# Layer-norm means, variances, reciprocal roots and shifts moved to GpSimd

## The chip, the cores and the metric

The kernel runs on one core of a Trainium2 chip. The metric is the device time of one launch in microseconds; the runs of the kernel before have a median of 207.16 us (206.71 to 207.61, two runs). The core has five engines that follow their own instruction queues in order and wait for each other by semaphores: TensorE (PE, matrix products), VectorE (DVE), ScalarE (ACT), GpSimd (POOL), and SyncE (SP), which issues the DMAs here.

## The reference

A block with a conditioned layer norm, a local dilated attention and a token-mixing MLP, on x of 2048 tokens by 512 channels in bf16. Shortened:

```python
def _layernorm(x, axis=-1, eps=1e-05):
    m = jnp.mean(x, axis=axis, keepdims=True)
    v = jnp.var(x, axis=axis, keepdims=True)
    return (x - m) / jnp.sqrt(v + eps)

mod = (silu(c) @ w_mod)            # six rows of 512: sa, ca, ga, sb, cb, gb
h = _layernorm(x) * (1 + ca) + sa                       # layer norm 1 (LN1)
x = x + ga * A(h, wqkv, wo)        # 32 heads of 16, 8 keys each, two tokens apart
h = _layernorm(x) * (1 + cb) + sb                       # layer norm 2 (LN2)
x = x + gb * B(h, w1, b1, w2, b2)

def B(x, ...):
    h = _layernorm(x)                                   # layer norm 3 (LN3)
    u = gelu(einsum('bsd,sf->bdf', h, w1) + b1)         # mixes the 2048 tokens, f = 1792
    return transpose(einsum('bdf,fs->bds', u, w2) + b2)
```

## The kernel before

The 2048 tokens are 16 tiles of 128 (token in the partition, 512 channels in the row), in five chunks of 2, 4, 4, 4 and 2 tiles (`SIZES`, so chunks begin at tiles 0, 2, 6, 10 and 14). For each chunk there is LN1, a transpose of the normalised tiles (by PE for the first two chunks, by DMA for the others: `xt`), the three projections (`qkv`, with evictions `ev`), the products of queries and keys on DVE (`qk`, four multiplies of 4096 columns for a chunk of four tiles), their sums by PE (`red`), a softmax (`max`, `sub`, `exp`, `esum`, `rcp`, `smB`), the products with the values on DVE (`pv`, four multiplies of the same size, summed by PE in `pvacc`), and the output projection with the residual (`wo`, `x1`). Then come LN2 (`n2_<tile>`), its affine part on DVE (`aff`, two multiplies or adds over the whole group) and LN3 (`h3_<tile>`). The products of `qk` and `pv` lie in four buffers named big, which `red` and `pvacc` release.

The MLP's first product (`mlp1_<sweep>_<feature tile>_<first token tile>`) sums over token tiles. It runs in sweeps over tiles 0 to 5, 6 to 10 and 11 to 15 for the feature tiles 0 to 6, and over tiles 0 to 9 and 10 to 15 for the feature tiles 7 to 13. A sweep's sums wait in `gT` (`park`, `inj`, `padd`) until the next. After GELU the second product (`mlp2`) and the output (`fin`, `st_out`) follow.

Each piece of work is added to a graph (`G.add`), with an engine, what it reads and what it writes. A list written out by hand, `ORDER`, gives the order in which all pieces are issued; so each engine's queue is the list's pieces of that engine, in the list's order. Nearly every instruction is issued through one helper, which is why the profile gives line 133 for all.

A layer norm's small work goes as follows. `ln_stats` (line 370) takes a tile's statistics: `bn_stats` and an aggregate on DVE (`ln1s`, `ln2s`, `ln3s`), or, for LN1 of tiles 10 to 13, two ACT sums and one DVE instruction (`ln1v`). LN2 of tiles 0 to 13 has its sums from ACT's `x1` and `ln2q`, and DVE makes the variance with two instructions (`ln2m`, line 869). `ln_rstd` (line 387) works on a group of tiles at a time: ACT takes Ln and Exp of the variance (`rstd`), DVE the shift (`nb`). A group is a whole chunk for LN1; for LN2 and LN3 it is 2, 2, 4, 1 and 1 tiles in the five chunks (`GRP`), and its name is that of its first tile (`rstd2_4`, `rstd3_4`). `ln_norm` (line 404) applies the scale and the shift on the engine that `NE` names for each tile, A for ACT, D for DVE, P for POOL:

```python
NE=('PAPAAPAADAAPAAPD', 'PAPAAPAAAADAAADP', 'APPAAADDDDADAADA'),
```

POOL has little else to do: constants and halos, two scalings of weights (`wsc2_2`, `wsc2_3`) and these normalisations. The parts of `ORDER` that matter most for the layer norms of the first tiles, of the first LN2 groups, and of the last tiles (lines 184, 208 to 209 and 222 to 224):

```
ln1s2 warm2 ld_wqkv0 silu_exp ld_wmod0 ln1s0 ln1s4 ln1s1 ln1s5 rstd1_0 ld_x_4_14 nb1_0 ln1s9 rstd1_1 n1_0 n1_1
...
warm3 n2_2 ev4_10:a ln3s0 wo6 a2_3_0 n2_3 ln3s1 a2_3_1 rstd2_4 wo7 x1_6 vd3_1 aff2 rstd3_0 a2_3_2 biascols wo9:q
ev4_20:a a2_3_3 nb2_4 nb3_0 ln3s3 n2_5 n2_4 vd3_2 warm1 ln3s2 h3_1 h3_0 qkv4_12 aff4 rstd3_2 wo8 x1_7 ld_w2_0
...
mlp1_0_13_0 aff10 oev4_0:a oev4_2:a aff13 mlp1_0_13_4 ln3s10 wo15 ld_w2_5 ln3s13 rstd3_10 mlp1_0_13_8 wo14 x1_15
rstd3_13 park0_12:a inj1_0 nb3_13 ln2s15 mlp1_1_0_6 nb3_10 x1_14 rstd2_15 mlp1_1_4_6 park0_13:a nb2_15 ln2s14
n2_15 inj1_3 inj1_6 ld_w1_1_896 inj1_5 mlp1_1_6_6 rstd2_14 aff15 h3_10 mlp1_1_3_6 ln3s15 mlp1_1_6_10 ln3s11
```

Of the kernel before, what the change touches and what calls it, by code (L numbers as in the profile page):

```python
# [8 lines left out]
ALU = mybir.AluOpType  # L9
BF = mybir.dt.bfloat16  # L10
F32 = mybir.dt.float32
PSUM = bass.MemoryType.PSUM
# [7 lines left out]
EPS = 1e-5  # L20
MASKVAL = -1.0e9
# [161 lines left out]
consts ld_x_1_2 act_table ld_x0 ld_x_1_4 ld_c ld_x_2_8 ld_x1 ident ld_x_2_6 ld_wmod1 ln1s3 halo0 ld_wqkv1 cps  # L183
ln1s2 warm2 ld_wqkv0 silu_exp ld_wmod0 ln1s0 ln1s4 ln1s1 ln1s5 rstd1_0 ld_x_4_14 nb1_0 ln1s9 rstd1_1 n1_0 n1_1
silu_dve nb1_1 ld_wqkv2 ln1s8 fill:2:70 tr0_0 n1_2 n1_4 modcols1 ln1s7 hT0_3:a n1_5 n1_3 ld_x_3_10 hT0_2:d a1col
hT0_0:a fill:4:16 tr1_2 wsc1_2:d ld_b1 hT0_1:a wsc1_3:d wsc1_0:a tr1_0 wsc1_1:d ln1s6 hT1_2:a ld_wmod2 qkv0_10
ld_x_3_12 wsc0_0:d rstd1_2 wsc0_1:d qkv0_12 wsc0_2:d hT1_1:a nb1_2 n1_8 n1_9 wsc0_3:d modcols0 hT1_0:d ld_wmod3
hT1_3:a qkv0_00 sab ev0_12:d n1_6 ld_wmod4 qvb0 ln1s14 ld_wo1 qkv0_02 qvb_cp0 ln1s15 ev0_00:a wsc2_2 qvb1
wsc2_0:d qkv1_00 wsc2_3 ev0_10:a ev0_02:d ln1s10 wsc2_1:d qkv1_10 qvb_cp1 qk0_0 ev1_10:a qkv0_22 qk0_1 n1_7
qkv0_20 ln1s13 qk0_2 qkv1_02 xt6 red0_0 ev1_00:a qk0_3 red0_1 red0_2 ev0_22:a ld_wmod5 qkv1_22 qk1_0 ev0_20:a  # L190
qkv1_12 ev1_02:a vd0_1 red0_3 ev1_12:a mask qkv1_11 vd0_0 ln1s11 max0 xt8 qk1_2 qkv1_01 ev1_11:a sub0 qkv1_03
ev1_01:a xt9 exp0 qkv1_13 qk1_1 ev1_03:a xt7 esum0 ev1_13:a qkv1_20 rcp0 vd0_2 ln1s12 qkv1_21 smB0 qk1_3 a2_0_3
modcol2 rstd1_4 qkv1_23 a2_0_0 ev1_22:a a2_0_2 halo_v1:a red1_0 ev1_20:a a2_0_1 red1_1 ln1v10 ln1v12 ln1v11
ln1v13 nb1_4 red1_2 rstd1_3 n1_15 ld_wo3 red1_3 nb1_3 ld_wo2 mcols0 n1_11 n1_10 qkv2_00 max1 ev1_21:a n1_14 xt10
qkv2_02 ev2_00:a pv0_0 qkv2_10 n1_12 ld_wo0 pv0_1 qkv2_11 vd0_3 ev2_10:a ev2_02:a qkv2_12 qk2_0 n1_13 qkv2_01
xt12 ev2_12:a pvacc0_0 ev2_01:a sub1 qk2_2 xt13 qkv2_03 exp1 qkv2_13 xt11 ev2_11:a ev2_03:a qkv2_22 qk2_1
ev2_13:a esum1 ev1_23:a qkv2_21 rcp1 vd1_2 red2_0 smB1 ev2_21:a ld_b2 red2_1 qk2_3 halo_v2:a a2_1_1 red2_2
pvacc0_1 a2_1_3 qkv3_00 a2_1_2 qkv3_10 a2_1_0 pv0_2 mrowt0 vd1_1 qkv2_20 ev3_10:a pv0_3 ev3_00:a red2_3 mrows0:a
qkv2_23 ev2_20:a st_row0 max2 halo_k3:p ev2_22:a vd1_3 qkv3_11 qk3_0 xt14 qkv3_22 ev3_11:a pvacc0_2 ld_row0
pvacc0_3 sub2:q oev0_2:a vd1_0 pv1_2 qkv3_02:q exp2 qkv3_12 ev3_02:a ev2_23:a qkv3_01 pv1_3 oev0_0:a vd2_2 esum2  # L200
modcol3 xt15 rcp2 ev3_12:a woq_s qkv3_20 ev3_01:a pvacc1_3 smB2 ev3_20:a red3_0 qk3_1 ev3_22:a a2_2_0 pvacc1_2
wo1 a2_2_1 vd2_3 qkv3_13:q x1_1 a2_2_2 pv1_1 vd2_1 wo0 ev3_13:a a2_2_3 qkv4_02 ld_w1_0_512 oev1_2:a mcols1 pv1_0
ld_w1_0_0 oev1_3:a mrowt1 qkv3_03 mrows1:a x1_0 st_row1 qkv4_00 ev3_03:a vd2_0 ln2q1 qk3_2 pvacc1_0 ev4_02:a
red3_1 pvacc1_1 oev1_0:a qkv3_23:q oev1_1:a qk3_3 ev4_00:a wo3:q ln2q0 wo5:q pv2_2 qkv4_22:q x1_5 ev3_23:a wo2:q
ld_row1 ln2q5 ld_w1_0_896 ln2m0 halo_v3:a wo4:q x1_3 pv2_1 x1_2 red3_2 x1_4 red3_3 ln2q3 qkv3_21:q pv2_3 rstd2_0
qkv4_20 ln2q2 ev3_21:a ev4_22:a vd3_3 pvacc2_1 nb2_0 max3 pvacc2_2 n2_0 warm0 ln2q4 vd3_0 n2_1 ln2m2 sub3 pv2_0
pvacc2_3 oev2_2:a exp3 rstd2_2 esum3 oev2_1:a aff0 pvacc2_0 rcp3 oev2_0:a qkv4_10 oev2_3:a ln2m4 nb2_2 smB3
warm3 n2_2 ev4_10:a ln3s0 wo6 a2_3_0 n2_3 ln3s1 a2_3_1 rstd2_4 wo7 x1_6 vd3_1 aff2 rstd3_0 a2_3_2 biascols wo9:q
ev4_20:a a2_3_3 nb2_4 nb3_0 ln3s3 n2_5 n2_4 vd3_2 warm1 ln3s2 h3_1 h3_0 qkv4_12 aff4 rstd3_2 wo8 x1_7 ld_w2_0
nb3_2 ln3s5 h3_3 h3_2 ln2q6 ln3s4 mlp1_0_6_0 ev4_12:a pv3_0 mlp1_0_3_0 x1_9 rstd3_4 mlp1_0_5_0 x1_8 mlp1_0_0_0  # L210
biascols_cp:a ln2q8 nb3_4 pv3_1 halo_v4:a mlp1_0_2_0 h3_4 vd4_1 h3_5 mlp1_0_1_0 ln2q9 pv3_2 ld_w2_1 mlp1_0_2_4
vd4_2 ln2q7 mlp1_0_0_4 vd4_0 mlp1_0_3_4 park0_0:a mlp1_0_1_4 mlp1_0_5_4:q park0_1:a ln2m6 vd4_3 pv3_3 park0_2:a
pvacc3_0 pvacc3_1 oev3_0:a ld_w1_0_1152 pvacc3_2 oev3_1:a mlp1_0_4_0:q rstd2_6 oev3_2:a qk4_2 pvacc3_3 park0_3:a
mlp1_0_7_0 oev3_3:a nb2_6 qk4_1 n2_6 mlp1_0_6_4 mlp1_0_4_4 n2_8 qk4_0 wo12:q ld_w1_0_1408 n2_7 n2_9 qk4_3 wo10:q
park0_4:a aff6 x1_12 red4_0 wo13:q ld_w2_3 park0_5:a ln2q12 red4_1 red4_2 x1_10 red4_3 wo11:q max4 ln2q10 ln3s9
x1_13 sub4:q mlp1_0_8_0:q exp4 ln3s8 ln2q13 mlp1_0_11_0 esum4 ln3s7 rcp4 mlp1_0_12_0 park0_6:a ln3s6 x1_11
mlp1_0_10_0 smB4 rstd3_6 ln2m12 a2_4_2 mlp1_0_9_0 h3_7 rstd2_12 h3_6 a2_4_3 ln2q11 h3_9 mlp1_0_8_4 ln2m13 a2_4_0
nb2_12 ln2m11 n2_12 mlp1_0_7_4 a2_4_1 ln2m10 h3_8 rstd2_10 ld_w2_4 aff12 mlp1_0_9_4 rstd2_13 rstd2_11 nb2_10
ln3s12 mlp1_0_9_8 mlp1_0_7_8 n2_10 mlp1_0_8_8 nb2_13 pv4_0 park0_7:a mlp1_0_12_4 ld_w1_0_1664 park0_8:a
mlp1_0_11_4 nb2_11 pv4_2 n2_13 mlp1_0_10_4 rstd3_12 pv4_1 park0_9:a mlp1_0_12_8 n2_11 mlp1_0_10_8 pv4_3 inj1_4  # L220
mlp1_0_11_8 ld_w1_1_0 park0_10:a pvacc4_2 ld_w1_1_640 park0_11:a pvacc4_0 nb3_12 aff11 pvacc4_1 h3_12 pvacc4_3
mlp1_0_13_0 aff10 oev4_0:a oev4_2:a aff13 mlp1_0_13_4 ln3s10 wo15 ld_w2_5 ln3s13 rstd3_10 mlp1_0_13_8 wo14 x1_15
rstd3_13 park0_12:a inj1_0 nb3_13 ln2s15 mlp1_1_0_6 nb3_10 x1_14 rstd2_15 mlp1_1_4_6 park0_13:a nb2_15 ln2s14
n2_15 inj1_3 inj1_6 ld_w1_1_896 inj1_5 mlp1_1_6_6 rstd2_14 aff15 h3_10 mlp1_1_3_6 ln3s15 mlp1_1_6_10 ln3s11
mlp1_1_0_10 rstd3_15 inj1_1 mlp1_1_1_6 park1_0:a nb3_15 h3_15 n2_14 rstd3_11 aff14 mlp1_1_5_6 h3_13 ln3s14
mlp1_1_5_10 mlp1_1_1_10 inj1_2 ld_w1_2_0 mlp1_1_2_6 h3_11 rstd3_14 park1_1:a h3_14 mlp1_1_4_10 mlp1_1_3_10
mlp1_1_2_10 mlp1_1_9_10 park1_2:a ld_w1_1_1408 park1_3:d mlp1_1_7_10 padd1_9 park1_4:a park1_5:d mlp1_1_8_10
padd1_7 gelu7 mlp1_1_10_10 park1_6:a mlp1_2_2_11 ld_w1_2_640 padd1_10 mlp1_2_2_14 mlp1_2_0_11 padd2_2
mlp1_2_0_14 ld_w2_7 gelu2 mlp1_2_1_11 padd2_0 mlp1_2_1_14 gelu0 mlp1_1_12_10 padd2_1 gelu10 padd1_8 gelu1
# [4 lines left out]
st_out5_0 fin8_0 mlp2_2_0 fin9_0 mlp2_13_0 fin2_0 st_out9_0 st_out8_0 st_out2_0 fin7_0 mlp2_10_0 fin13_0  # L234
st_out7_0 fin6_0 mlp2_12_0 st_out6_0 st_out13_0 mlp2_11_0 fin12_0 fin10_0 st_out12_0 mlp2_14_0 st_out10_0
fin11_0 st_out11_0 mlp2_15_0 fin14_0 mlp2_15_1 st_out14_0 fin15_0 mlp2_15_2 fin15_1 st_out15_0 st_out15_1
fin15_2 st_out15_2
# [4 lines left out]
def kernel(  # L242
# [92 lines left out]
    epscol = T([P, 1], F32, "epscol")  # L335
# [17 lines left out]
    for l in range(3):  # L353
        for nm, n in (("st6", 6), ("mv", 2), ("lv", 1), ("rs", 1), ("nb", 1)):
            ln_t[nm, l] = T([P, NST, n], F32, f"{nm}_{l}")
# [14 lines left out]
    def ln_stats(l, st, src, reads, name):  # L370
        st6, mv = ln_t["st6", l], ln_t["mv", l]
        if l == 0 and st in LN1A:
            def fa():
                nc.scalar.activation(junk[:], src, ACT.Identity, scale=1.0 / D, accum_out=mv[:, st, 0:1])
                nc.scalar.activation(junk[:], src, ACT.Square, scale=D ** -0.5, accum_out=st6[:, st, 0:1])
            add("act", 1.36, fa, reads=reads + ["act_table"], writes=[("sq", l, st)], name=name)
            add("dve", 0.15, lambda: nc.vector.scalar_tensor_tensor(
                mv[:, st, 1:2], mv[:, st, 0:1], mv[:, st, 0:1], st6[:, st, 0:1], op0=ALU.mult, op1=ALU.subtract,
                reverse1=True), reads=[("sq", l, st)], writes=[("mv", l, st)], name="ln1v" + name[4:])
            return  # L380

        def fd():
            nc.vector.bn_stats(st6[:, st, :], src)
            nc.vector.bn_aggr(mv[:, st, :], st6[:, st, :])
        return add("dve", 0.86, fd, reads=reads, writes=[("mv", l, st)], name=name)

    def ln_rstd(l, g0, n, name, var=None, vreads=None):
        mv, lv, rs, nb = (ln_t[k, l] for k in ("mv", "lv", "rs", "nb"))
        sl = slice(g0, g0 + n)
        var = mv[:, sl, 1] if var is None else var  # L390
# [648 lines left out]
```

## Time and profile before

| what | value |
|---|---|
| median of the runs (two) | 207.16 us |
| span of the profiled execution | 204.6 us |
| time of the runs less that span | 2.6 us |
| PE busy | 194.7 us (95%) |
| DVE busy | 163.3 us (80%), 260 instructions |
| ACT busy | 120.6 us (59%), 283 instructions |
| POOL busy | 13.0 us (6%), 36 instructions |
| granted TensorE clock, mean | 0.998 |

The small work of the layer norms in the profile's groups: 30 aggregates on DVE (182 ns each), 16 instructions of `ln2m` and 4 of `ln1v` (151 to 210 ns), 21 of `nb` (145 to 159 ns); on ACT 25 Ln (289 to 298 ns) and 25 Exp (203 to 207 ns). A normalisation of a tile takes 0.77 us on POOL, 0.80 on ACT and 0.40 on DVE.

In the lines of the profile, times are in microseconds from the start of the span; a line of the timeline gives the start, the length, the engine, the line of the kernel, the operation, what is written <- what is read, the shapes, how many instructions are merged (x), and in brackets how long the engine had been idle and for what it waited. Tiles carry the program's names: `st` are the statistics, `mv` mean and variance, `lv` the logarithm, `rs` the reciprocal root, `nb` the shift, `xx` the residual, `h` the normalised tiles, `psS` and `psL` PSUM, `wst` the streamed weights, `lsb` the softmax, `vD` and `a2sb` the operands of `pv`.

### The profile page before, as it was taken

The page shows a single profiled execution, that of the slowest core. Times are in us where ns is not written, and L with a number is a line of the kernel's source. Part 1 is how long each engine was busy: PE and PEld are TensorE (multiplying, and loading weights), DVE is VectorE, ACT ScalarE, POOL GpSimd, SP SyncE. Part 2 cuts the span into 40 slices and gives each one's busy share as a digit, 9 for nine tenths or more (in the row PEclk, how much of TensorE's full clock was granted, in tenths as well). Part 3 has the DMA queues.
Part 4 walks back from the last instruction along what each step waited for, and adds up shares of the span by engine and source line. Part 5 has one row for each costly group of instructions (what it writes and reads, how often), then busy time and mean ns, then how long its engine had stood idle before and what let it go on. Part 6 is the DMA issues. An engine that isn't in the chain of part 4 may idle for free.

```text
span 204.6 us, 4223 instructions
## 1 busy us (share of the span) xinstructions
PE 194.7 (95%) x1655; PEld 103.5 (51%) x1655; DVE 163.3 (80%) x260; ACT 120.6 (59%) x283; POOL 13.0 (6%) x36
## 2 busy tenths in 40 slices
PE   3999999999999997989899999999999999999994
PEld 3988554454455553554344445444444444444453
DVE  2899999999999999999999999975473204369365
ACT  2398998994666899989898876683762000000000
POOL 4122001100000001240000000100000000000000
PEclk9999999999999999999999999999999999999999
DMA  5999494646958976194975179946990930121121
GB/s 141 330 380 348 117 239 107 161 98 201 247 186 267 308 234 251 25 272 110 289 200 115 26 157 263 288 131 200 340 304 3 232 88 16 39 77 51 51 82 51
DMA packets 55111, 35.93 MB, mean 176 GB/s; under 512 B 24628, under 2 KB 52404, under 8 KB 55092
## 3 DMA queue, kind: packets, MB, share of 16 engines
q1 hardware_dynamic: 55084, 35.67, 61.4%
q8 instruction: 13, 0.21, 0.4%
q14 instruction: 6, 0.05, 0.1%
q10 hardware_dynamic: 8, 0.00, 0.0%
HBM read 22.55 MB, written 2.10 MB: 121 GB/s over the span
## 4 chain that ended last, share of the span: by engine, by line
PE 65%; DVE 20%; issue 5%; DMA 5%; SPq 3%; ACT 2%; DVEq 0%
PE psS L133 62%; DVE big L133 9%; DVE h L133 3%; PE psL L133 3%; SPq L133 3%; DVE st L133 3%; DMA wst<-in_B_w_dram 2%; DMA xx<-in_A_x_dram 2%; ACT h L133 1%; DVE mv L133 1%; DVE m L133 1%; DVE lsb L133 1%; DVE ls L133 0%; DVE nb L133 0%; DVE woq L133 0%
## 5 line engine op out<-in xcount | busy, mean ns | idle before, releaser
L133 PE MATMUL psS<-h,wst 128*128 128x512 bf16 (+1 forms) x254 | 50.7, 379 | 1.2 <-POOL h L133 0.7
L133 PE MATMUL psS<-hT,w_qkv 128*128 128x512 bf16 (+3 forms) x312 | 46.2, 339 | 0.3 <-ACT w_qkv L133 0.3
L133 PEld LDWEIGHTS <-wst 128*128 128x128 bf16 (+1 forms) x356 | 28.7, 98 | 32.2 <-issue 3.2
L133 PEld LDWEIGHTS <-w_qkv 128*128 128x128 bf16 (+1 forms) x354 | 29.5, 111 | 21.3 <-issue 3.2
L133 DVE TENSOR_TENSOR big<-a2sb,vD 128x4096 bf16<-128x4096 bf16 (+1 forms) x20 | 36.9, 1876 | 0.0
L133 DVE TENSOR_TENSOR big<-q_sb,k_f 128x4096 bf16<-128x4096 bf16 (+1 forms) x20 | 36.3, 1857 | 0.0
L133 DVE SCALAR_TENSOR_TENSOR h<-psS,bcol,rows_bc 128x512 f32<-128x512 f32 (+2 forms) x18 | 12.4, 690 | 24.4 <-PE psS L133 24.2
L133 PE MATMUL psS<-gT,big 128*128 128x512 bf16 x112 | 24.8, 379 | 0.0
L133 PEld LDWEIGHTS <-big 128*128 128x128 bf16 x144 | 12.0, 97 | 13.2
L133 PEld LDWEIGHTS <-ident 128*128 128x128 bf16 (+1 forms) x203 | 13.9, 111 | 5.9 <-issue 2.8
L133 PE MATMUL psS<-woq,o_sb 128*32 128x512 bf16 (+1 forms) x172 | 16.6, 380 | 0.0
L133 ACT ACTIVATE h<-xx,nb,rs 128x512 bf16<-128x512 bf16 x19 | 15.0, 807 | 0.8 <-DVE nb L133 0.7
L133 DVE TENSOR_TENSOR psS<-psS,gT 128x512 f32<-128x512 f32 x14 | 9.3, 696 | 7.0 <-PE psS L133 7.0
L133 ACT ACTIVATE junk<-xx 128x512 bf16<-128x512 bf16 x22 | 13.8, 626 | 0.2
L133 POOL TENSOR_SCALAR h<-xx,rs,nb 128x512 bf16<-128x512 bf16 x9 | 7.3, 813 | 101.3 <-DVE nb L133 84.0
L133 ACT ACTIVATE lv<-mv,epscol 128x1 f32<-128x1 f32 (+2 forms) x25 | 7.3, 291 | 9.3 <-DVE mv L133 8.4
L133 DVE BATCH_NORM_STATS2 st<-xx 128x6 f32<-128x512 bf16 x14 | 9.5, 678 | 4.0 <-DMA xx<-in_A_x_dram 4.0
L133 ACT ACTIVATE gT<-psS,bcol 128x512 bf16<-128x512 f32 x14 | 8.7, 688 | 6.4 <-DVE psS L133 6.4
L133 PEld LDWEIGHTS <-group 128*32 128x32 bf16 x288 | 6.8, 96 | 10.2 <-issue 4.8
L133 DVE TENSOR_TENSOR h<-h,rows_bc 128x512 bf16<-128x512 bf16 (+2 forms) x20 | 11.5, 581 | 0.5
L133 DVE TENSOR_TENSOR h<-h,xx 128x512 bf16<-128x512 f32 (+2 forms) x18 | 11.4, 633 | 0.6
L133 ACT ACTIVATE gT<-psS 128x512 bf16<-128x512 f32 x19 | 10.8, 587 | 1.6 <-PE psS L133 1.5
(94 smaller groups left out, 220.4 us busy)
## 6 DMA issues: line engine op xcount, KB each, us to landing
vD<-v_sb SPq DMA_DIRECT2D x12, 524.5 KB, 3.8
big<-in_B_w_dram SPq DMA_DIRECT2D x4, 896.0 KB, 8.2
vD<-v_sb SPq DMA_DIRECT2D x8, 268.5 KB, 3.0
wst<-in_B_w_dram SPq DMA_DIRECT2D x3, 640.0 KB, 5.3
out_dram<-h SPq DMA_DIRECT2D x15, 128.0 KB, 1.8
xx<-in_A_x_dram SPq DMA_DIRECT2D x7, 256.0 KB, 6.1
wst<-in_B_w_dram SPq DMA_DIRECT2D x2, 800.0 KB, 4.8
gT<-in_w_mod_dram SPq DMA_DIRECT2D x3, 512.0 KB, 6.1
```

What stands on the lines that cost most here:

```text
L133: r = fn(*a, **k)
```

## The change

The aggregates, `ln1v`, `ln2m`, `nb` and ACT's Ln and Exp go. `ln_stats` only takes the raw statistics, and `ln_rstd` issues for each group 16 instructions on POOL (14 where the statistics are sums): mean and variance, the shift's first factor, a seed of the reciprocal root by integer arithmetic on the number's bits, two Newton steps of four instructions each, and the shift. All work on 1 to 4 columns of float32. The normalisations stay on the engines that `NE` names, and all of them now use scale and shift. `ORDER` loses the names that are gone, and nothing in it moves.

```diff
     def ln_stats(l, st, src, reads, name):
...
-        def fd():
-            nc.vector.bn_stats(st6[:, st, :], src)
-            nc.vector.bn_aggr(mv[:, st, :], st6[:, st, :])
-        return add("dve", 0.86, fd, reads=reads, writes=[("mv", l, st)], name=name)
+        return add("dve", 0.66, lambda: nc.vector.bn_stats(st6[:, st, :], src), reads=reads, writes=[("st", l, st)],
+                   name=name)
...
-        def fa():
-            nc.scalar.activation(lv[:, sl, 0], var, ACT.Ln, bias=epscol[:, 0:1])
-            nc.scalar.activation(rs[:, sl, 0], lv[:, sl, 0], ACT.Exp, scale=-0.5)
...
+    def ln_rstd(l, g0, n, name, kind):
+        st6, sm, mv, rs, nb = (ln_t[k, l] for k in ("st6", "sm", "mv", "rs", "nb"))
         sl = slice(g0, g0 + n)
+        g = nc.gpsimd
+
+        def f():
+            if kind == "bn":
+                g.tensor_tensor(mv[:, sl, 0], st6[:, sl, 1], st6[:, sl, 4], op=ALU.subtract)
+                g.tensor_tensor(sm[:, sl, :], st6[:, sl, 1:3], st6[:, sl, 4:6], op=ALU.add)
+                g.tensor_tensor(mv[:, sl, 0], mv[:, sl, 0], mv[:, sl, 0], op=ALU.mult)
+                g.tensor_scalar(mv[:, sl, 1], sm[:, sl, 1], 4.0 / D, 4.0 * EPS, op0=ALU.mult, op1=ALU.add)
+                first, neg, k = sm[:, sl, 0], -0.5, 2.0
+            else:
+                neg, k = (-1.0 if l == 0 else -1.0 / D), 1.0
+                first = sums[:, sl, 0]
+                g.tensor_tensor(mv[:, sl, 0], first, first, op=ALU.mult)
+                g.tensor_scalar(mv[:, sl, 0], mv[:, sl, 0], -neg * neg, EPS, op0=ALU.mult, op1=ALU.add)
+            second = mv[:, sl, 1] if kind == "bn" else sums[:, sl, 1]
+            g.tensor_tensor(mv[:, sl, 0], mv[:, sl, 0], second, op=ALU.add)
+            g.tensor_scalar(nb[:, sl, 0], first, neg, 0.0, op0=ALU.mult, op1=ALU.add)
+            v, y, t = mv[:, sl, 0], rs[:, sl, 0], mv[:, sl, 1]
+            g.tensor_scalar(y.bitcast(I32), v.bitcast(I32), -0.5, RSQRT_SEED, op0=ALU.mult, op1=ALU.add)
+            for it in range(2):
+                g.tensor_tensor(t, y, y, op=ALU.mult)
+                g.tensor_tensor(t, t, v, op=ALU.mult)
+                last = k if it == 1 else 1.0
+                g.tensor_scalar(t, t, -0.5 * last, 1.5 * last, op0=ALU.mult, op1=ALU.add)
+                g.tensor_tensor(y, y, t, op=ALU.mult)
+            g.tensor_tensor(nb[:, sl, 0], nb[:, sl, 0], rs[:, sl, 0], op=ALU.mult)
...
+        add("pool", 1.5, f, reads=keys, writes=[("rs", l, g0), ("mv", l, g0)], name="rstd" + name)
```

The number 1.5 in the last line is the length that the graph notes for a piece; the order does not follow from it, since `ORDER` gives that.

## The prediction

> **What bounds the kernel now.** First the page's busy row and its slices.
>
> ```profile
> PE 194.7 (95%) x1655; PEld 103.5 (51%) x1655; DVE 163.3 (80%) x260; ACT 120.6 (59%) x283; POOL 13.0 (6%) x36
> ...
> DVE  2899999999999999999999999975473204369365
> ACT  2398998994666899989898876683762000000000
> POOL 4122001100000001240000000100000000000000
> ```
>
> TensorE (PE) is busy nearly always; VectorE (DVE) is full until about 135 us; GpSimd (POOL) is almost free. Second the chain that ended last, in order of time:
>
> ```profile
> 7.33 0.70 DVE st L133
> ...
> 13.61 9.50 PE psS L133 x108
> ...
> 112.83 88.75 PE psS L133 x465
> ```
>
> The first projection matmul starts at 13.61, once the layer norms of the first tiles are through. From 112.83 PE never waits again. Whatever makes PE wait is therefore paid in full, and little can be gained: in the timeline PE's visible waits after 14 us add up to about 3.5 us (0.74, 0.57, 0.22, 0.68, 0.73 and 0.52).
>
> Third, DVE beside POOL in the timeline:
>
> ```profile
> 36.28 1.57 DVE L133 TENSOR_TENSOR big<-a2sb,vD 128x2048 bf16<-128x2048 bf16 x1
> 37.77 1.22 DVE L133 TENSOR_TENSOR big<-a2sb,vD 128x2048 bf16<-128x2048 bf16 x1
> 83.77 0.68 DVE L133 TENSOR_TENSOR lsb<-lsb,rb 128x1024 bf16<-128x1024 bf16 x1
> 83.95 1.15 POOL L133 TENSOR_SCALAR h<-xx,rs,nb 128x512 bf16<-128x512 bf16 x1 [4.48 <-DVE nb L133]
> ```
>
> POOL's normalisation, elsewhere 0.77 us, took 1.15 when it came 0.18 us after a DVE multiply had begun: it ended 0.65 after the multiply did. The DVE multiply of 36.28, normally 1.22, took 1.57 while POOL was busy until 36.78. So a DVE multiply of two SBUF operands and a POOL instruction do not run together; one waits for the other to end.
>
> **What is removed.** DVE loses 30 aggregates, 4 of ln1v, 16 of ln2m and 21 of nb. An aggregate (0.182 us, overlapping its neighbour) costs some 0.2 of DVE time: 6.0. ln2m is 8 pairs of 0.35 (2.8), ln1v 4 x 0.13 (0.5), nb 21 x 0.09 (1.9): 11.2 us, of which about 7.5 before 112 us. ACT loses 25 pairs of 0.5, 12.5 us. PE can use no more than the 3.5 us it waits. One small constant fill (0.10) goes too. At nothing I cost DVE's normalisations, which change form (0.402 and 0.404 us in the two forms of now), and ACT's sums of tiles 10 to 13, which only write elsewhere. No DMA is added, and none changes its queue.
>
> **What is added.** 16 POOL instructions for a group with bn_stats, 14 for one with sums. LN1 has 4 of the first and 1 of the second, LN2 2 and 8, LN3 10: 382 instructions of 1 to 4 columns where POOL now runs 36. In a bn group 13 stand in one dependent line (difference, square, sum, seed, 8 Newton instructions, last product); the others lie beside it but for some 0.06 us. A sums group has 13 in line too.
>
> The price of a step is the open number. The trace has no small two-operand instruction on POOL. The nearest rows:
>
> ```profile
> 1.00 0.21 POOL L133 TENSOR_SCALAR_AFFINE_SELECT group<-group 128x32 bf16<-128x32 bf16 x1
> 1.28 0.21 POOL L133 TENSOR_SCALAR_AFFINE_SELECT group<-group 128x32 bf16<-128x32 bf16 x1
> ...
> 2.98 0.10 POOL L133 MEMSET epscol<- 128x1 f32 x1
> ```
>
> The two selects depend on each other: 0.28 from start to start, 0.07 more than one takes. At 128 columns a select takes 0.29, so a column costs 0.0008, and one of one column would be spaced 0.26. A fill of one column, which reads nothing, takes 0.10, with the same 0.07 0.17. Independent fills of a few columns start 0.035 apart; that is the bottom if steps did not wait for each other. The new instructions read like a select but evaluate no index pattern. I take **0.23**, nearer the select; the ends are 0.035 and 0.30 (a select with a little for a second operand). A bn group is then 13 x 0.23 + 0.06 = 3.05 us, a sums group 3.0. The path it replaces takes 1.06 from the last bn_stats to nb (8.02 to 9.08 for rstd1_0).
>
> The Trainium skill (GPSIMD Engine Reference, Elementwise — side-by-side cycle accounting) has a two-operand add on GpSimd 1.96 times as long as on VectorE and so speaks against the move; no row here shows it. Twice the 0.15 us of DVE's small rows would be 0.30, with the gap 0.37, for the 10 of 13 steps with two operands, and the sum below would end near 280: an estimate.
>
> **The walk.** POOL runs its queue in the order list's order, so a normalisation on POOL also waits behind chains that are not its own. A time and its row of before stand side by side. Beside back-to-back DVE multiplies I give a chain one step for each multiply.
>
> *Start.* Statistics at 8.02. rstd1_0 from 8.1 to 11.15, rstd1_1, ahead of n1_0 in the queue, to 14.2, n1_0 (0.77) to 14.97; before, 9.96. The transposes of the first chunk wait for n1_0, DVE's n1_8, and wsc0_3 behind it, for rstd1_2 (19.6 against 14.92). **+5.0** on PE's first projection.
>
> *rstd1_3.* ACT's n1_10 waits for it, and ev2_00, on which DVE's qk2_0 depends, is behind n1_10. It gets 7 steps by the end of max1, 2 at pv0_0 and pv0_1, and 4 while DVE stands: qk2_0 at 45.8 against 38.91, **+2.0** more (7.0).
>
> *First LN2 groups, 70 to 92 us of before.* rstd2_0: DVE's four multiplies of 2.2 us pass 4 steps, max3 (from PSUM) 4 to 5, pv2_0 one; the last 4 run with DVE standing. aff0 8.1 late (**+1.1**). rstd2_2: 3 steps beside aff0 and smB3, 5 beside bn_stats, 5 alone: aff2 9.3 late (**+1.2**). rstd2_4 has 6 left when DVE is free; then the queue has the whole of rstd3_0 (3.05) ahead of n2_5 (0.77), for which aff4 waits: 14.05 late (**+4.8**). rstd3_2: 4 to 5 steps beside bn_stats, 4 beside pv3_0 to pv3_3 (8.8 us), the rest alone, as DVE then lacks big buffers, whose release stands behind mlp1 in PE's order; h3_2 0.77. PE waits there even now:
>
> ```profile
> 91.52 1.67 PE L133 MATMUL psS<-h,wst 128*128 128x512 bf16 x7 [0.68 <-POOL h L133]
> ```
>
> It starts at 116.3: **+10.7** (24.8 in all).
>
> *Third chunk.* rstd3_4 hides behind ACT's evictions (h3_4 comes 3.5 us after h3_3 now too). rstd2_6 loses 4 multiplies of qk4: aff6 **+1.5**. aff6 to the last ln3s is 6.2 us, without aggregates; rstd3_6 ends **+1.5** (27.8), at 141.7.
>
> *Last six tiles.* Groups of one tile: POOL has 12 more chains in a row, rstd2_12, 10, 13, 11, rstd3_12, 10, 13, rstd2_15, 14, rstd3_15, 11, 14. They are 12 x 3.03 = 36.4 us, 1.9 for the four pv4 multiplies, 0.8 for n2_15, 1.4 for affine multiplies, 0.4 for h3_14: 182.6, with some 1.5 for data arriving from DVE and ACT 184. Before, rstd3_6 to h3_14 is 113.90 to 136.26, 22.4. **+20**. PE's mlp1_1_9_10 needs all six tiles and runs at once after h3_14; about 66 us of PE work remain.
>
> Sum 5.0 + 2.0 + 1.1 + 1.2 + 4.8 + 10.7 + 1.5 + 1.5 + 20 = 47.8. The profiled execution spans 204.6, so 252.4; the runs shown have a median of 207.16, 2.6 above that span, so **255**. A step is paid some 235 times along the way (25 at the start, 45 in the middle, 165 at the end), so 0.01 us of its price is 2.35 us of time. DVE's 11 us saved lie in DVE time spent standing.
>
> PE's granted clock is 1.00 in every stretch of the windows view, which holds no long PE pause. The Trainium skill (TensorE: Matmul & The Clock Gate, Part 1) says that the clock halves after an idle window of about 3.4 us; pauses as long as mine are not in this trace, and by the rule some 2 to 5 us would come on top.
>
> **Rivals.**
> - *Dearer step*, 0.27 to 0.34 (two operands read one after the other): 255 + 235 x 0.04 to 0.11 = 264 to 281. For it: nothing here reads two operands. Against: the select is probably the heavier instruction.
> - *Cheaper step*, 0.10 to 0.19 (a fill's own length, with or without a gap): 224 to 246. For it: the one-column fill. Against: the gap of dependent selects.
> - *The port matters less*: small instructions slip in beside DVE multiplies. The 4 multiplies of rstd3_2 would cost 0 instead of some 7 us, qk4, pv4 and the first ones some 6 more: 242. Against: the two rows above.
> - *Not slower*: POOL streams these steps 0.035 apart, like independent fills. A chain is then 13 x 0.035 = 0.5 us, under the 1.06 it replaces; DVE's 7.5 us before 112 remain as a gain, PE closes its 3.5 us: 203.7, within 2%. It decides once a chain stays under 1.06, 0.08 a step. Against: every new step reads what the one before wrote, and the selects show that such steps wait.
>
> **How the numbers follow.** Likeliest, 0.19 to 0.27 a step with the port as shown, 246 to 264: 0.50. Dearer 0.18, cheaper 0.17, the port 0.08, not slower 0.07. The range 224 to 283 takes in a step from 0.10 to 0.35 and leaves out the last case and tails. A measurement of this kernel tells about 2% from no change. Faster by over 2% would need more than PE's visible waits, 0.03; within 2% 0.04; slower 0.93.
>
> **What would show it.** POOL's row should have some 400 instructions and 60 to 100 us busy. n1_0 should end near 15; DVE's row should show gaps before every affine multiply of 70 to 185 us, ended by POOL or by ACT waiting for POOL; the last unbroken PE stretch should begin near 184. I am wrong if steps of one chain start less than 0.10 apart, if chains run on beside DVE multiplies, or if the last stretch still begins near 136.

## The result, and the profile after

The changed kernel takes 275.81 us (median; 274.66 to 276.95) against 207.16: a ratio of 1.331, 95% interval 1.316 to 1.346. The prediction was 255, range 224 to 283; the time lies within the range, but above the band called likeliest (246 to 264) and in that of the dearer step (264 to 281). The profiled execution spans 272.9 us, 68.3 more than before. The page of the changed kernel, its busy row, two slice rows and the chain that ended last:

```profile
PE 210.7 (77%) x1635; PEld 108.2 (40%) x1655; DVE 157.3 (58%) x189; ACT 110.4 (40%) x233; POOL 121.4 (45%) x417
...
DVE  3534988799999843790286271543223553047765
...
POOL 3665846500037887997402787777750000000000
...
PE 44%; POOL 33%; issue 8%; DVE 4%; SPq 4%; ACT 4%; DMA 2%; POOLq 0%; DVEq 0%; ACTq 0%
```

DVE lost its 71 small instructions and only 6 us of busy time, and is no longer full: it stands. POOL went from 13 to 121 us of busy time (60 to 100 were forecast), and a third of the chain that ended last is now its work. A step alone, from the timeline of the last chain, rstd3_14:

```profile
200.12 0.19 POOL L135 TENSOR_TENSOR mv<-rs 128x1 f32<-128x1 f32 x1
200.39 0.19 POOL L135 TENSOR_TENSOR mv<-mv 128x1 f32<-128x1 f32 x1
200.67 0.19 POOL L135 TENSOR_SCALAR mv<-mv 128x1 f32<-128x1 f32 x1
200.95 0.19 POOL L135 TENSOR_TENSOR rs<-rs,mv 128x1 f32<-128x1 f32 x1
```

Each takes 0.19, and the next, which reads its result, starts 0.27 after it. A chain of 16 is 3.8 us. Beside DVE's multiplies it looks otherwise. Here is rstd3_2 on POOL, and DVE over the same stretch:

```profile
113.95 0.19 POOL L135 TENSOR_SCALAR rs<-mv 128x2 int32<-128x2 int32 x1
114.23 2.26 POOL L135 TENSOR_TENSOR mv<-rs 128x2 f32<-128x2 f32 x1
116.57 2.12 POOL L135 TENSOR_TENSOR mv<-mv 128x2 f32<-128x2 f32 x1
118.78 2.11 POOL L135 TENSOR_SCALAR mv<-mv 128x2 f32<-128x2 f32 x1
120.97 2.12 POOL L135 TENSOR_TENSOR rs<-rs,mv 128x2 f32<-128x2 f32 x1
123.17 0.19 POOL L135 TENSOR_TENSOR mv<-rs 128x2 f32<-128x2 f32 x1
```

```profile
112.96 1.29 DVE L135 BATCH_NORM_STATS2 st<-h 128x6 f32<-128x512 bf16 x2
114.16 8.88 DVE L135 TENSOR_TENSOR big<-a2sb,vD 128x4096 bf16<-128x4096 bf16 x4
```

Four multiplies, four steps: one step gets through for each. ("The port" is the name used below for whatever it is that a DVE multiply of two SBUF operands and a POOL instruction can't use at once.) As soon as the fourth multiply ends, a step is 0.19 again. PE's line of the same place, with what it waited for, answers to the line of 91.52 before:

```profile
125.40 9.23 PE L135 MATMUL psS<-h,wst 128*128 128x512 bf16 x38 [12.41 <-POOL h L135]
```

The last unbroken stretch of PE, which began at 112.83 before, begins at 203, where the prediction had 184 (the chain in order of time):

```profile
202.53 0.42 DVE h L135
203.00 1.44 PE psS L135 x3
204.44 0.22 issue
204.66 12.44 PE psS L135 x49
...
217.15 10.74 PE psS L135 x49
```

### The profile page after: what moved, and what is told of

It reads as the page before. It is cut to its first block, busy times and chain, and to the rows that moved or that the text cites. A ratio compares the mean times of both kernels' runs of the same rounds, so it can differ in the third digit from the quotient of the medians.

```text
span 272.9 us, 4468 instructions
## 1 busy us (share of the span) xinstructions
PE 210.7 (77%) x1635; PEld 108.2 (40%) x1655; DVE 157.3 (58%) x189; ACT 110.4 (40%) x233; POOL 121.4 (45%) x417
## 4 chain that ended last, share of the span: by engine, by line
PE 44%; POOL 33%; issue 8%; DVE 4%; SPq 4%; ACT 4%; DMA 2%; POOLq 0%; DVEq 0%; ACTq 0%
PE psS L135 42%; POOL mv L135 20%; POOL rs L135 6%; SPq L135 4%; POOL nb L135 4%; DMA xx<-in_A_x_dram 2%; POOL h L135 2%; PE psL L135 2%; DVE big L135 2%; ACT q_sb L135 1%; POOL sm L135 1%; ACT junk L135 1%; DVE h L135 1%; DVE w_qkv L135 1%; ACT h L135 1%
## 5 line engine op out<-in xcount | busy, mean ns | idle before, releaser
L135 PE MATMUL psS<-h,wst 128*128 128x512 bf16 (+1 forms) x249 | 60.3, 423 | 32.7 <-POOL h L135 13.2
L135 PEld LDWEIGHTS <-wst 128*128 128x128 bf16 (+1 forms) x356 | 30.8, 104 | 71.7 <-issue 48.3
L135 PE MATMUL psS<-hT,w_qkv 128*128 128x512 bf16 (+3 forms) x305 | 48.4, 347 | 3.0 <-DVE w_qkv L135 2.2
L135 DVE TENSOR_TENSOR big<-q_sb,k_f 128x4096 bf16<-128x4096 bf16 (+1 forms) x20 | 36.7, 1874 | 13.7 <-ACT gT L135 11.9
L135 PE MATMUL psS<-gT,big 128*128 128x512 bf16 x111 | 24.8, 379 | 0.1
L135 POOL TENSOR_TENSOR mv<-mv 128x1 f32<-128x1 f32 (+2 forms) x82 | 21.0, 256 | 5.2
L135 POOL TENSOR_SCALAR mv<-mv 128x1 f32<-128x1 f32 (+2 forms) x59 | 16.7, 283 | 5.2
L135 POOL TENSOR_TENSOR mv<-rs 128x1 f32<-128x1 f32 (+2 forms) x50 | 17.0, 341 | 4.0
L135 ACT ACTIVATE h<-h,nb,rs 128x512 bf16<-128x512 bf16 x8 | 6.3, 808 | 28.0 <-POOL nb L135 28.0
L135 PEld LDWEIGHTS <-big 128*128 128x128 bf16 x144 | 12.1, 99 | 13.2
L135 POOL TENSOR_TENSOR rs<-rs,mv 128x1 f32<-128x1 f32 (+2 forms) x50 | 14.6, 293 | 4.2
L135 POOL TENSOR_TENSOR mv<-sums 128x1 f32<-128x1 f32 (+2 forms) x9 | 4.6, 507 | 25.1 <-ACT xx L135 19.8
L135 PE MATMUL psS<-big,group 128*32 128x512 bf16 (+1 forms) x160 | 10.5, 371 | 6.0 <-ACT gT L135 5.4
L135 ACT ACTIVATE gT<-psS 128x512 bf16<-128x512 f32 x19 | 10.7, 589 | 9.6 <-PE psS L135 9.6
```

The lines of the kernel that those rows point to most:

```text
L135: r = fn(*a, **k)
```

## The experiments

Each is timed against the kernel before on the same chip, whose medians there were 207.03 to 207.47. The changed kernel was not timed again there: where a run is compared with it, its 275.81 is meant, whose two runs lie 2.3 us apart.

**One part of the change at a time.** Three kernels with the change for some groups only; the others keep aggregate, Ln, Exp and shift as before.

```diff
+    POOLG=<the groups (layer, first tile) that go through GpSimd>,
...
+    def ln_stats(l, st, src, reads, name):
+        return (ln_stats_pool if on_pool(l, st) else ln_stats_old)(l, st, src, reads, name)
```

LN1 alone:

> Only LN1's five groups go through GpSimd; LN2 and LN3 stay on ACT and DVE. Theory (chains are serial time on GpSimd and are paid where PE or DVE wait for them): in the changed kernel the statistics of the first LN2 group are in 13 us later than before (83.6 against 70.6), all of it from LN1, so about 13 us over the kernel before, near 220. Rival (LN1 has slack and only LN2 and LN3 matter, as DVE's savings make up the rest): within 3 us of 207.

Measured: 221.41, ratio 1.069 (1.058 to 1.079): 13.9 more.

LN2 and LN3 of tiles 0 to 9:

> Only LN2 and LN3 of tiles 0 to 9 (eight chains) go through GpSimd. Theory: from the first LN2 group to the end of rstd3_6 the changed kernel loses 37.7 - 13 = 25 us against before, so 25 us more than before, near 232. Rival (the middle lost so much only because LN1 had upset the order of the engines): under 12 us.

Measured: 233.05, ratio 1.125 (1.118 to 1.132): 25.6 more.

LN2 and LN3 of tiles 10 to 15:

> Only LN2 and LN3 of tiles 10 to 15 (twelve chains of one tile) go through GpSimd. Theory: twelve chains of 3.8 us in a row against 22 us before: 29 us more than before, near 236; with the other two runs the three excesses add up to the whole, 67 to 69. Rival (the tail is late only because all before it is late, and PE has other work): under 10 us, and the three don't add up.

Measured: 231.56, ratio 1.118 (1.109 to 1.126): 24.1 more, 5 less than expected. All three rivals fall: each part is late by itself. The parts add up to 63.6 of the 68.7 that the medians differ by. The missing 5 is not clear of noise: the intervals of the four ratios together leave some 4.5 us open. If it is real, the profile has a place for it, since the parts share one queue. With the last six tiles alone, POOL takes up rstd2_12 when its first sum is in (the second line is the first step of the next chain, rstd2_10):

```profile
107.40 0.49 POOL L137 TENSOR_TENSOR mv<-sums 128x1 f32<-128x1 f32 x1 [15.40 <-ACT xx L137]
112.28 0.19 POOL L137 TENSOR_TENSOR mv<-sums 128x1 f32<-128x1 f32 x1
```

In that run ACT does rstd3_6, so it does not stand ahead in POOL's queue. In the whole change the sums for rstd2_12 are in at 142.85, but POOL has rstd3_6 ahead of it and starts it at 151.54.

**The length of a chain.** One Newton step instead of two:

```diff
-            for it in range(2):
+            for it in range(1, 2):
```

> The changed kernel with one Newton step instead of two: four instructions fewer in each of the 25 chains, so the reciprocal roots are less exact. Theory (a dependent step costs 0.273 us): 1.1 us a chain, about 23 chains on the path, 25 us less, near 251. Rival (the loss comes from DVE being held off by GpSimd at the port, or from the lower PE clock, not from the chains' length): under 8 us less.

Measured: 249.71 (ratio 1.205, 1.198 to 1.213), 26.1 less than the changed kernel. Four steps of 0.273 on the 23 chains that were expected on the path make 25.1, and the profiled span is 24.8 shorter: 5.2 of it lie ahead of the statistics of rstd2_0 (in at 78.4 instead of 83.6), 5.7 from there to PE's restart with h3_2 (114.47 instead of 125.40), 13.7 from there to the end of h3_14 (178.32 instead of 202.95). A step taken out of a chain on the path comes back in full as time of the kernel.

**What a step's price is made of.**

```diff
+            def beside():
+                i = next(side)
+                g.tensor_tensor(idle[:, i, sl], wide[:, sl], wide[:, sl], op=ALU.mult)
             for it in range(2):
                 g.tensor_tensor(t, y, y, op=ALU.mult)
+                beside()
                 g.tensor_tensor(t, t, v, op=ALU.mult)
+                beside()
...
```

> The changed kernel with 200 more GpSimd instructions: after each of the eight Newton instructions of a chain a multiply of the same size that depends on nothing. Theory (a step costs 0.273 because it waits for the one before; an independent instruction starts 0.15 after its forerunner): a pair takes 0.30 instead of 0.273, 0.25 us a chain, and beside DVE multiplies both go through the same gap: 5 to 8 us more, near 282. Rival (each GpSimd instruction of this kind costs some 0.27 us whatever it depends on): 2.2 us a chain on 23 chains, 50 us more, near 326.

Measured: 281.53, 5.7 more, with 200 instructions more. The timeline of a chain without multiplies beside it:

```profile
203.40 0.19 POOL L135 TENSOR_TENSOR mv<-rs 128x1 f32<-128x1 f32 x1
203.55 0.19 POOL L135 TENSOR_TENSOR idle<-wide 128x1 f32<-128x1 f32 x1
203.69 0.19 POOL L135 TENSOR_TENSOR mv<-mv 128x1 f32<-128x1 f32 x1
203.84 0.19 POOL L135 TENSOR_TENSOR idle<-wide 128x1 f32<-128x1 f32 x1
```

The instruction in between fits into the time in which the next step would wait. An instruction occupies POOL for 0.145 us; the price of 0.273 is the wait for the forerunner's result. The pair of a Newton step and an idle one takes 0.29 (203.40 to 203.69), as expected, and the rival falls.

**The number of chains.** Tiles 10 to 15 in pairs. Out of `ORDER` go the second tile's pieces (rstd2_13, rstd2_11, rstd2_15, rstd3_13, rstd3_11, rstd3_15, aff11, aff13, aff15), and n2_13, ln3s13, ln3s11, rstd2_14, ln3s15 and h3_15 move to where a pair is complete:

```diff
-    GRP=(2, 2, 4, 1, 1),
+    GRP=(2, 2, 4, 2, 2),
```

> The changed kernel with tiles 10 to 15 in three groups of two instead of six of one, and the order list mended for it: six chains instead of twelve in the tail. Theory (a chain's cost does not depend on its columns): 6 x 3.8 = 23 us less, and 2 to 4 us back because a group waits for both tiles: 255 to 258. Rival (the tail's time goes with the tiles, or with DVE's and ACT's work on them): within 5 us of the changed kernel.

Measured: 259.35 (ratio 1.251, 1.245 to 1.257), 16.5 less, a little short of the 255 to 258 expected. The mechanism holds, but what comes back by waiting was put too low: the tail (end of rstd3_6 to the last normalised tile) fell from 51.4 to 35.1 us, by 16.3 and not by 23. POOL, which never stood in the tail of the changed kernel, now waits for both tiles' statistics ahead of the last two chains, rstd2_14 and rstd3_14:

```profile
175.80 0.20 POOL L135 TENSOR_TENSOR mv<-st 128x2 f32<-128x2 f32 x1 [2.15 <-DVE st L135]
183.50 0.28 POOL L135 TENSOR_TENSOR mv<-st 128x2 f32<-128x2 f32 x1 [2.85 <-DVE st L135]
```

That is 5.0 us. The multiplies of pv4 cost a little more than in the changed kernel: they meet rstd3_12 (8.3 us instead of 3.8), where they met rstd2_13 (7.2 instead of 3.6).

**The port.** The four multiplies beside rstd3_2 made short, so that three quarters of their products are left out:

```diff
+                    n = C // 4 if ch == 3 else C
-                    nc.vector.tensor_tensor(pv(), a2sb.unsqueeze(2).to_broadcast([P, 2, 4, C]),
...
+                    nc.vector.tensor_tensor(pv()[:, :, :, 0:n], a2sb[:, :, 0:n].unsqueeze(2).to_broadcast([P, 2, 4, n]),
...
```

> The changed kernel with the four value multiplies of the fourth chunk (pv3_0 to pv3_3) over a quarter of their columns; the rest of their products is left out. In the changed kernel four steps of rstd3_2 lie beside them and take 2.2 us each. Theory (one step gets through for each DVE multiply): these steps shrink to some 0.6 us, rstd3_2 from 12.1 to 5.5 to 6 us, PE restarts 6 us earlier, and the time falls by 5 to 7 us. Rival (the steps are slow there for another reason): rstd3_2 stays near 12 us and the time moves by less than 2 us.

Measured: 269.79 (ratio 1.302, 1.292 to 1.312), 6.0 less. POOL's timeline, over the same four steps as above:

```profile
115.21 0.66 POOL L135 TENSOR_TENSOR mv<-rs 128x2 f32<-128x2 f32 x1
115.95 0.52 POOL L135 TENSOR_TENSOR mv<-mv 128x2 f32<-128x2 f32 x1
116.56 0.51 POOL L135 TENSOR_SCALAR mv<-mv 128x2 f32<-128x2 f32 x1
117.16 0.52 POOL L135 TENSOR_TENSOR rs<-rs,mv 128x2 f32<-128x2 f32 x1
```

The steps shrink with the multiplies, rstd3_2 takes 5.7 us instead of 12.1, and PE restarts with h3_2 at 119.98 instead of 125.40. The rival falls.

**The order of POOL's queue.**

```diff
-rstd1_0 ld_x_4_14 ln1s9 rstd1_1 n1_0 n1_1
+rstd1_0 ld_x_4_14 ln1s9 n1_0 rstd1_1 n1_1
...
-aff2 rstd3_0 a2_3_2 ... ln3s3 n2_5 n2_4
+aff2 n2_5 rstd3_0 a2_3_2 ... ln3s3 n2_4
```

> The changed kernel with two places of the order list altered: rstd1_1 behind n1_0, and n2_5 ahead of rstd3_0, so that neither normalisation waits for a chain that is not its own. Theory A (GpSimd's total work up to h3_2 and up to rstd1_2 decides, and the order of its queue shifts it only a little): 2 us at the start and 2 to 3 in the middle, near 271. Theory B (as in the prediction's walk, the foreign chain ahead is the loss: 3 at the start, 4.8 for aff4): 7 to 8 us less, near 268 or below.

Measured: 276.42, ratio 1.334 (1.320 to 1.347): nothing won. Both theories are wrong: neither the 7 to 8 us of B nor the 4 to 5 of A came. In the middle n2_5 and aff4 came as hoped (aff4 at 108.75 instead of 111.12), so DVE reached its multiplies earlier and they met rstd3_0:

```profile
111.58 2.17 POOL L135 TENSOR_SCALAR mv<-mv 128x2 f32<-128x2 f32 x1
113.83 2.12 POOL L135 TENSOR_TENSOR rs<-rs,mv 128x2 f32<-128x2 f32 x1
116.03 2.12 POOL L135 TENSOR_TENSOR mv<-rs 128x2 f32<-128x2 f32 x1
118.23 2.12 POOL L135 TENSOR_TENSOR mv<-mv 128x2 f32<-128x2 f32 x1
```

rstd3_0 took 12.6 us instead of 3.8, rstd3_2 3.9 instead of 12.1, and h3_2 ended at 126.8 instead of 125.4. At the start n1_0 ended 3.8 us earlier, but the timeline shows DVE waiting in front of hT0_2 nearly as long as in the changed kernel (7.20):

```profile
17.64 0.29 DVE L135 COPY hT<-psS 128x256 bf16<-128x256 bf16 x1 [7.00 <-ACT hT L135]
```

ACT's hT0_3 stood behind n1_4, which needs rstd1_1. Moving n1_4 and n1_3 behind the evictions should show it:

```diff
-hT0_3:a n1_5 n1_3 ... hT0_2:d a1col hT0_0:a ... tr1_2 ... hT0_1:a
+hT0_3:a n1_5 ... hT0_2:d a1col hT0_0:a hT0_1:a n1_4 n1_3 ... tr1_2
```

> The changed kernel with the order list altered at the start alone: rstd1_1 behind n1_0 on GpSimd, and n1_4 and n1_3, which wait for rstd1_1, behind the evictions hT0_3, hT0_0 and hT0_1 on ACT. Theory (in the run with rstd1_1 behind n1_0 nothing was won because n1_4 stood ahead of hT0_3 on ACT, and DVE's hT0_2 and with it ln1s6, the last statistics for rstd1_2, waited there): ln1s6 is in near 16 instead of 19.5, rstd1_2 starts when GpSimd is through with n1_5, near 18, instead of 19.6, n1_8 starts 1.5 us earlier, and the time falls by 1 to 2 us. Rival (something else holds ln1s6): ln1s6 stays at 19.5 and the time within 0.5 us.

Measured: 275.63 and 271.39. Two runs so far apart give no time for this kernel. The start of the profiled one, 275.63, can still be read: ln1s6 is in at 15.5 (19.8 in the changed kernel), rstd1_2 starts at 17.98 behind n1_5, and n1_8 at 21.97 instead of 24.06.

```profile
13.59 0.29 DVE L135 COPY hT<-psS 128x256 bf16<-128x256 bf16 x1 [3.09 <-ACT hT L135]
...
21.97 0.79 DVE L135 TENSOR_SCALAR h<-xx,rs,nb 128x512 bf16<-128x512 bf16 x1 [5.73 <-POOL nb L135]
```

So the wait named was the right one, and n1_8 comes 2.1 us earlier. What this is worth in time is left open.

**The clock after a pause.** The changed kernel with 200 small matmuls ahead of mlp1_1_9_10, so that PE does not stand there:

```diff
+fill:9:200 mlp1_1_9_10
```

> The changed kernel with 200 small matmuls of the identity (about 11.4 us at full clock, into PSUM that nobody reads) ahead of mlp1_1_9_10, where PE stands from 189.6 to 202.5 but for a few matmuls. Theory (after that pause PE's clock is granted at 0.50 until about 208, and some 2.4 us are lost): the clock stays at 1.00 through the restart, and from h3_14's end to the end of the span it takes 67.5 to 68.5 us instead of 69.95 (before: 68.3). Rival (the restart is slow because of something else): 69.5 or more.

Inconclusive: 276.93, and 70.2 us from h3_14's end to the end. The chains came 3 us later in this execution, and the fill ran out at 201.4 before h3_14 ended at 206.1. The granted clock in the windows view (it stands behind the five engines' busy times):

```profile
190.00:200.00 10.00, 10.00 (x177) 9.86 (x176) 4.12 (x8) 1.94 (x4) 7.79 (x42) 1.00 0.43 141
200.00:206.00 6.00, 2.59 (x33) 1.79 (x30) 0.76 (x3) 2.32 (x4) 4.23 (x23) 0.91 0.00 0
206.00:208.00 2.00, 1.88 (x5) 0.71 (x5) 1.49 (x4) 0.00 (x0) 0.00 (x0) 0.50 0.00 0
```

It was 1.00 while the fill ran, and 0.50 again after less than 5 us with only four matmuls. So this run does not separate what the low clock costs. The other traces come closer. In the changed kernel the first 49 matmuls in a row after h3_14 took 12.44 us, each later 49 took 10.74, and the granted clock was 0.50 until about 208. With the change for the last six tiles alone the clock was back near 164, and the same 49 took 11.64; with the first ten alone the clock stayed at 1.00 there, and they took 10.74. From the end of h3_14 to the end of the span these runs took 69.95, 69.15 and 68.3 (before: 68.3). From these numbers 1.7 us is an estimate of what the low clock costs at this restart; the runs differ in more than the clock.

**Where a chain has time.** The kernel before, with one and two late groups on GpSimd.

```diff
+    POOLG=((0, 14),),                # late_one
+    POOLG=((0, 10), (0, 14)),        # late_two; n1_10 and xt10 behind ev2_00
```

> The kernel before with one group alone on GpSimd: LN1 of tiles 14 and 15, whose statistics are in at 18 us and whose first user runs at 34.5. Theory (a chain costs nothing where some 16 us lie between its statistics and its first user, even beside DVE multiplies): DVE loses two aggregates and a shift, 0.5 us, ACT 0.5 us, and the time falls by 0 to 0.5 us against the kernel before. Rival (GpSimd's steps hold DVE's multiplies off at the port): 0.5 to 1.5 us more than before.

Measured: 206.64 against 207.03, ratio 0.998 (0.996 to 1.001): the rival's loss of 0.5 us or more lies outside the interval; the gain of up to 0.5 can't be told from nothing.

> The kernel before with LN1 of tiles 14 and 15 and of tiles 10 to 13 on GpSimd, n1_10 and its transpose moved behind ev2_00 in the order list. Theory: DVE loses about 1.1 us of small instructions before 35 us; rstd1_3 ends near 37 instead of 35 and n1_10 no longer has ACT's evictions behind it, so the time falls by 0.3 to 1 us. Rival (rstd1_3 runs into the multiplies from 36 us on, ends 4 us or more late, and the third chunk's evictions wait on ACT behind n1_12): 1 to 3 us more than before.

Measured: 209.60, ratio 1.011 (1.008 to 1.015): the rival is right, and there is a further cause that it did not name. rstd1_4 stands ahead in the queue and ends only at 34.5, as it lies beside the multiplies of qk0 and qk1, so rstd1_3 starts then; two of its steps meet pv0 (1.25 and 1.04 us), and it ends at 40.2, 5 us late. No version here beats the kernel before by more than the measurement can tell.

## Why the prediction was right, and where it was off

The mechanism was right in kind and place: dependent steps on POOL, priced by their number, and paid where PE waits. The size of the step was not, and nearly every term came out too small. The delays below are differences between the two profiled executions at the prediction's own landmarks.

| term | predicted | measured |
|---|---|---|
| start (n1_8) | 5.0 | 9.1 |
| rstd1_3 (to the statistics of rstd2_0) | 2.0 | 3.9 |
| aff0, aff2, aff4 | 1.1, 1.2, 4.8 | 1.2, 2.7, 5.2 |
| PE's restart with h3_2 | 10.7 | 11.7 |
| aff6, rstd3_6 | 1.5, 1.5 | 0.8, 3.1 |
| last six tiles (h3_14) | 20 | 29.0 |
| PE after h3_14 | 0 | 1.6 |
| sum | 47.8 | 68.3 |

*The step's price* is the term that was mis-sized: 0.273 against 0.23. I had corrected the dependent selects to 0.26 for one column and then went below them, because the new instructions evaluate no index pattern. That reason was wrong: in the chains a difference, a product, a scaling with two constants and the seed in integers all take 0.18 to 0.20 us when nothing lies beside them, and all are waited for alike. At 235 steps the 0.043 make 10 us of the 20.5 missing. The instructions that lie beside the line cost more as well: I gave them 0.06 us for a chain, but each occupies POOL for 0.145. Together a chain of 16 takes 3.8 us instead of 3.05, one of 14 takes 3.6 instead of 3.0. The last six tiles have eight of the one and four of the other: 8 x 0.75 + 4 x 0.6 = 8.4 of the 9.0 missed there. It is the low end of the rival "dearer step" (0.27), to which the prediction gave 0.18, though not for its reason: instructions with one operand and with two take the same 0.19 here. The rival "cheaper step" (0.10 to 0.19) falls with the same number.

*The start* was the second miss. I had seen that wsc0_3 stood behind n1_8, but took the statistics of rstd1_2 as in by then. They are late: hT0_2 stands ahead of ln1s6 on DVE and waits for ACT's hT0_3, which stands behind n1_4. rstd1_2 began at 19.87, not at 16.5. The next term, *rstd1_3*, is not a matter of its steps beside multiplies either: there was one and not two, but the chain began only at 42.65, after POOL had stood 5.3 us for ACT's sums.

*The foreign chains ahead of n1_0 and n2_5*, which the walk names as causes (3 us, and most of the 4.8), were not the whole cause. Taking them away by themselves won nothing, as the next wait stood right behind.

*The port* behaved as the two rows of before showed, down to one step for each multiply: the walk had rstd3_2 with 4 steps beside pv3 and the chain has 4. The rival "the port matters less" falls by the run with the short multiplies. The rival "not slower" falls by the step of 0.273, and the run with the independent instructions shows why it could not hold: POOL starts even those 0.145 apart and not 0.035.

*DVE's 11 us saved* show as only 6.0 in its busy time; where the rest is stays open. As foreseen, the saving went into time spent standing.

*The rules of the Trainium skill.* In the GPSIMD Engine Reference (Elementwise — side-by-side cycle accounting) a two-operand add takes 1.96 times as long on GpSimd, measured at 2048 columns. At 1 to 4 columns no such ratio is seen here: 0.19 us, against 0.15 to 0.16 on DVE. By luck the estimate from it, 280, was nearer than mine. TensorE: Matmul & The Clock Gate (Part 1) says that the clock halves after an idle window. This agrees with the changed kernel's windows: PE stood from 189.6, the granted clock was 1.00 until about 194.4 and 0.50 from then on, and only four matmuls ran in the 13 us before 203:

```profile
203.00:205.00 2.00, 1.78 (x4) 0.71 (x5) 1.49 (x3) 0.00 (x0) 0.00 (x0) 0.50 0.00 0
...
209.00:211.00 2.00, 2.00 (x11) 0.93 (x10) 0.70 (x1) 0.00 (x0) 0.00 (x0) 1.00 0.18 33
```

The granted clock stays at 0.50 until about 208. From h3_14 to the end it takes 1.6 us more than before, a little under the 2 to 5 us noted. The clock was 0.50 in other stretches too (118 to 125, where PE stood, and 170 to 180, where it was busy for 7.2 us), its mean fell from 0.998 to 0.881, and PE's busy time rose by 16.0 us; what that costs ahead of h3_14 no run separates.

## What to carry to other kernels

A chain of tiny dependent instructions cost here about its number of steps times the wait between two of them (0.273 us), not the work in them: a chain of 3.8 us in place of a path of 1.06, taken by 25 groups in one in-order queue, added a third to the kernel's time. Count the steps of a chain, price one by the nearest dependent pair in the trace and do not go below it, and add one DVE multiply for each step that lies beside back-to-back DVE multiplies of two SBUF operands. When a wait is taken away on paper, look what stands right behind it in each queue: time that two pieces of work cannot share only moves from one to the other.

## What was not expected of the hardware

A GpSimd instruction on one column and one on four take the same time (0.19 to 0.20 us), with one operand or two, and one that waits for no result starts 0.145 us after its forerunner. DVE is held off too: the normalisation n1_8, 0.41 us before, took 0.78 beside POOL's wsc2_2. And with the 200 small matmuls PE's clock fell to 0.50 at about 205, 3.5 us after the last of them and only 1.9 us after the last of four matmuls that followed.
